# A cross-attention and maxout kernel: the head in another order, batch 3's x issued later, state reads turned behind the weights

## The chip, the cores and the metric

The kernel runs on one core of a Trainium2 chip. The metric is device time in microseconds (us), the median of several runs. Engines are named as the profile names them: PE (matmuls; PEld is its weight load), DVE (vector), ACT (scalar), POOL and SP. DMAs are issued from POOL, ACT and SP. The kernel keeps 8 PSUM banks: four singles (`b0` to `b3`) and two pairs (`w0`, `w1`).

## The reference

Inputs: `x` (8, 8, 512, 64) and `state` (8, 8, 32, 64), batch, head, row, depth; weights `w1`, `w2`, `w3` (512, 768) and `w_out` (768, 512). In float32:

```python
scores = scale * x @ state.T                    # (B, H, 512, 32), scale = 1/8
a = softmax(scores, -1);  xread = a @ state     # rows of x read the state
scores2 = scale * state @ x.T                   # (B, H, 32, 512)
a2 = softmax(scores2, -1); sread = a2 @ x       # rows of the state read x
t = concat([xread, sread], 2)                   # (B, H, 544, 64)
t = t.transpose(0, 2, 1, 3).reshape(4352, 512)  # one token per row
h = max(max(t @ w1, t @ w2), t @ w3)            # maxout, 768 wide
out = h @ w_out                                 # (4352, 512)
```

## The kernel before, in words

Matmuls run in bf16. The 512 x rows of a batch need no product of their own with the state's values: since `xread @ w = a @ (state @ w)`, the kernel forms `G = state @ w` once a batch (32 rows a head, 3 x 768 columns) and then layer 1 as `G` times the turned softmax weights. The 32 state rows of all batches go through layers 1 and 2 together at the end (`"s"`).

The steps of the program are written by hand as a text, step by step; `perform` runs through it and calls one function a step. Within an engine, instructions run in this written order; between engines they wait for one another by semaphores. In the old kernel there are three texts, `FIRST` (head and batches 0 and 1), `EACH` (once for each of five batches) and `LAST`. Two more strings, `BANKS` and `PAIRS`, give the PSUM bank of each product in turn. The steps, with the lines of their instructions:

- `lst k q`: state of batches 2k and 2k+1 from HBM (L152, 128 KB) on queue `q`. `stc`, `stt`, `stp`: cast it (L217), turn it on PE (L222), place it block-diagonally (L228).
- `lxg b g`, `lx b`: half or all of the x of a batch (L168, L163), cast to bf16 under way, on POOL's queue. `lxu`, `cxu`: the first half uncast on SP's queue, cast by DVE (L176).
- `lw m0 m1 i`: columns 128 x m0 to 128 x m1 of weight i (0 for w1, 1 for w2, 2 for w3), cast under way, on POOL's queue (L179); 128 KB in bf16 for each 128 columns. `lwo`: w_out (L184, 768 KB).
- `busy`: a matmul of zeros (L211) that fills PE's wait at the start.
- `xt`/`xtc`: turn x on PE and copy it (batches 0 and 1, L237, L244); `xtd`: turn x by DMA on SP (L249). `sc`: scores (L262, tile `ps`), `ex`: exponentials on ACT (L269), `sum`: sums and reciprocals on DVE (L276, L278), `wt`: softmax weights (L284) on POOL (P) or DVE (D). `at`/`atc`: turn the weights on PE (L295, tile `pat`) and copy them (L298); `atd`: the same by DMA on SP (L302).
- `pad b`: x beside a column of ones on POOL (L308, L311), used by `sr`, the state read (L327, tile `psr`); `srs`: its division (L337 to L343); `srt`: its turn by DMA on SP (L346); `ap`: its place among the state tokens (L351).
- `g b m`, `gc`: a slice of G on PE, 128 columns of each of the three weights (L363, tile `pg`, 8 matmuls), and its copy (L381). `gr`, `grc`: a run of G columns instead (L403, L406).
- `l1 b m`: a block of layer 1 (L416, three products `pw` of two matmuls, one per weight). `m0`, `ma`, `mb`: copy of the first (ACT, L431), maximum with the second and the third (DVE, L436, L440).
- `l2 b j`, `l2c`: layer 2 (L447, tile `po`, 6 matmuls) and its copy to `osb` (L454); `so`: store (L477). `l2p`, `l2pc`, `sop`: parts of these in the last stage (L462, L466, L472).
- `ones`: a constant, behind a copy that waits for w_out (L194, L195). `look`, `flag`, `vl`, `hold`: a test of the sums that decides on a second pass, which is not run here.

Slice m of G needs the weight columns of slice m from all three weights; `l1 b m` needs that slice and the turned weights of the batch. Each transfer on POOL's queue also waits, before it is issued, for the eighth before it to land.

A batch in the loop is one pass of `EACH`: the runs of G and the scores of the next batch stand between the blocks of layer 1 of this one and layer 2 of the one before.

Of the kernel before, what the change touches and what calls it, by code (L numbers as in the profile page):

```python
# [17 lines left out]
FIRST = """  # L18
    lst 0 A; lxu 0 0 S; zero; clr 0; clr 1; clr 2; clr 3; warm; lxg 0 1; busy 1; xones 1; ident; busy 1;
    lxg 1 0; busy 1; busy 1; stc 0 D; busy 1; busy 1; busy 1; busy 1; busy 1; lxg 1 1; stt 0; busy 2;  # L20
    cxu 0 0 D; xt 0 0; stp 0 A; busy 1; xt 0 1; busy 1; xtc 0 0 D; lw 0 2 1; lw 0 2 2; xtc 0 1 D;
    busy 1; sc 0 0; busy 1; lw 0 1 0; busy 1; sc 0 1; lw 1 3 0; ex 0 0; busy 1; busy 1; xt 1 0; sum 0 0;
    lw 2 3 1; busy 1; ex 0 1; sum 0 1; xt 1 1; busy 1; xtc 1 0 AD; busy 1; lw 2 3 2; busy 1; xtc 1 1 A;
    busy 1; wt 0 0 P; wt 0 1 P; xones 0; sc 1 0; ex 1 0; busy 1; sc 1 1; at 0 0; atc 0 0 A; sr 0;
    busy 1; sum 1 0; lw 3 4 0; at 0 1; lst 1 A; lw 3 6 2; lw 3 6 1; ex 1 1; wt 1 0 D; g 0 0; gc 0 0 D;
    busy 1; sum 1 1; g 1 0; sr 1; atc 0 1 A; lw 4 6 0; wt 1 1 P; at 1 0; srs 0; g 1 1; g 0 1; stc 1 P;
    l1 0 0; gc 1 1 D; gc 1 0 A; g 1 2; g 0 2; atc 1 0 A; busy 1; gc 0 1 A; m0 0 0; at 1 1; lxg 2 1;
    srs 1; ma 0 0; l1 0 1; lxg 2 0; gc 0 2 A; l1 0 2; atc 1 1 D; l1 1 0; m0 0 1; m0 0 2; lwo; m0 1 0;
    gc 1 2 A; mb 0 0; xtd 2; l1 1 1; g 0 3; m0 1 1; lst 3 S; lst 2 A; ma 0 1; gc 0 3 A; g 1 3; pad 2;
    stt 1; gc 1 3 A; mb 0 1; ma 0 2; mb 0 2; ma 1 0; mb 1 0; l1 1 2; ma 1 1; g 0 5; m0 1 2; ones; g 0 4;  # L30
    mb 1 1; stp 1 DA; l1 0 3; gc 0 4 A; ma 1 2; g 1 4; gr 2 1792 2304; gc 0 5 D; m0 0 3; mb 1 2; l1 1 3;
    l1 0 5; gc 1 4 A; gr 2 0 512; g 1 5; m0 1 3; ma 0 3; mb 0 3; ma 1 3; l1 1 4; grc 2 1792 2304 A;
    mb 1 3; m0 0 5; gr 2 1280 1792; stc 2 P; lxg 3 1; gr 2 512 1024; ma 0 5; l1 0 4; stt 2; sc 2 -;
    gc 1 5 A; m0 1 4; grc 2 0 512 D; mb 0 5; lxg 3 0; ma 1 4; grc 2 1280 1792 AD; m0 0 4; ma 0 4;
    mb 0 4; mb 1 4; xtd 3; l2 0 3; l2 0 1; ex 2 -; l1 1 5; stp 2 A; l2c 0 3 D; stc 3 P; l2 0 2; sum 2 -;
    l2c 0 1 D; stt 3; l2 0 0; m0 1 5; ma 1 5; l2c 0 2 A; grc 2 512 1024 D; wt 2 - P; sr 2; mb 1 5;
    srs 2; gr 2 1024 1280; l2c 0 0 D; so 0 0 2 P; lx 4; so 0 2 4 P; stp 3 A; grc 2 1024 1280 A; atd 2;
"""
EACH = """
    pad 1; gr 1 1792 2304; gr 1 0 512; grc 1 1792 2304 AD; l2 -1 0; l2 -1 1; l1 0 0; grc 1 0 512 D;  # L40
    l2c -1 0 A; m0 0 0; sc 1 -; l2 -1 3; gr 1 1024 1280; ex 1 -; xtd 2; gr 1 1280 1792; l2c -1 1 D;
    ma 0 0; gr 1 512 1024; mb 0 0; sr 1; grc 1 1024 1280 A; l1 0 1; l1 0 2; sum 1 -; l1 0 3; srs 1;
    l1 0 5; l2c -1 3 A; m0 0 1; m0 0 2; ma 0 1; mb 0 1; ma 0 2; m0 0 3; mb 0 2; srt -2; ma 0 3;
    wt 1 - P; m0 0 5; mb 0 3; l2 -1 2; grc 1 1280 1792 A; grc 1 512 1024 A; ma 0 5; mb 0 5; l2c -1 2 D;
    l1 0 4; so -1 2 4 P; m0 0 4; ma 0 4; lx 3; mb 0 4; atd 1; ap -2 A; so -1 0 2 P;
"""
LAST = """
    srt 6; l1 7 0; srt 7; l2 6 0; l1 7 2; m0 7 0; l1 7 3; l1 7 4; ap 7 D; m0 7 2; srt 5; ap 6 A; ma 7 0;
    m0 7 3; mb 7 0; ap 5 A; l2c 6 0 D; ma 7 2; l2 6 1; l1s 0; l2 6 2; m0 7 4; mb 7 2; l1 7 1; l2c 6 1 A;
    ma 7 3; m0 s 0; l2c 6 2 A; l1s 2; l1 7 5; ma 7 4; mb 7 4; look; ma s 0; m0 7 1; m0 s 2; mb s 0;  # L50
    so 6 2 3 S; m0 7 5; mb 7 3; l1s 1; ma 7 1; mb 7 1; ma s 2; mb s 2; ma 7 5; m0 s 1; ma s 1; l1s 5;
    so 6 0 1 S; mb 7 5; l2p 7 2 384 512; l1s 3; m0 s 5; ma s 5; mb s 1; m0 s 3; mb s 5;
    l2pc 7 2 384 512 A; l2p 7 0 384 512; l2p 7 3 256 512; sop 7 2 384 512 P; ma s 3; l2p 7 2 128 384;
    mb s 3; l2p 7 0 0 128; l2pc 7 0 0 128 A; l2pc 7 3 256 512 D; l2p 7 1 0 128; l2p 7 3 0 256;
    l2pc 7 0 384 512 D; flag; l2pc 7 1 0 128 A; l2pc 7 2 128 384 A; l1s 4; m0 s 4; l2 6 3;
    sop 7 0 0 128 P; ma s 4; sop 7 0 384 512 P; mb s 4; l2p s 0 256 512; so 6 1 2 P; l2 s 1;
    sop 7 3 256 512 A; l2c 6 3 D; l2p 7 2 0 128; sop 7 1 0 128 S; l2p s 0 0 256; so 6 3 4 A;
    l2pc 7 3 0 256 D; l2pc s 0 256 512 D; sop s 0 256 512 A; l2pc 7 2 0 128 A; l2p 7 1 128 384;
    sop 7 2 0 128 A; l2p 7 0 256 384; l2p 7 1 384 512; l2pc s 0 0 256 A; l2p 7 0 128 256;
    l2pc 7 1 128 384 A; l2c s 1 D; sop 7 3 0 256 S; sop 7 2 128 384 P; l2pc 7 0 256 384 D;  # L60
    sop 7 1 128 384 A; l2pc 7 1 384 512 D; sop 7 1 384 512 A; l2pc 7 0 128 256 D; sop 7 0 128 256 A;
    sos 1 S; sop s 0 0 256 S; sop 7 0 256 384 S; hold; vl;
"""

BANKS = """
# [10 lines left out]
def kernel(  # L76
# [60 lines left out]
    def new(d, b, shape, name, bufs=2):  # L137
        d[b] = work.tile(shape, BF16, tag=name, bufs=bufs, name=name)
# [539 lines left out]
```

## Time and profile before

| what | value |
|---|---|
| runs | 152.47, 152.57, 152.87 us; median 152.57 us |
| span of the profiled execution, first to last instruction | 151.4 us |
| what the median has beyond that span | 1.17 us; the profiled execution's own time is its span and about as much around it |
| PE busy | 146.4 us (97%) |
| DVE, ACT, POOL busy | 118.9 (79%), 82.8 (55%), 57.0 us (38%) |
| DMA moved | 22.29 MB |
| granted TensorE clock | 1.000 |

All waits, chains and rows in this document come from one profiled execution. In the chain, each entry is what released the next one, so the entries of PE that follow each other without another engine between them are PE working at its own pace. "PE pg L363 x16" is sixteen matmuls of line 363. Idle time of other engines counts only where the chain passes through them.

### The profile page before, as it was taken

Reading aid. Unit: us, or ns where it says so; the run is one execution under the profiler, and the core shown is the slowest. Engines: PE = TensorE matmul, PEld = TensorE weight load, DVE = VectorE, ACT = ScalarE, POOL = GpSimd, SP = SyncE. Lnnn points to the kernel's source line nnn. Section 1 sums busy time; section 2 is a strip of 40 time slices with the busy share of each in tenths; the row PEclk is TensorE's granted clock in tenths of the full one; section 3 lists DMA queues with packets and bytes.
Section 4 is the critical chain, followed back from the end, with each engine's and each line's share of the span. In section 5 each row is a group of like instructions: output and inputs, shape, how many; then the busy total and the mean of one; then the engine's idle time right before and its main releaser. Section 6 shows DMA issues by size and latency. Waiting matters only on the chain.

```text
span 151.4 us, 3635 instructions
## 1 busy us (share of the span) xinstructions
PE 146.4 (97%) x1431; PEld 73.8 (49%) x1431; DVE 118.9 (79%) x204; ACT 82.8 (55%) x143; POOL 57.0 (38%) x79
## 2 busy tenths in 40 slices
PE   6999799999999999999999999999999999999992
PEld 2566343335445443544354435443544446679771
DVE  6477698999977898879987988798879887675353
ACT  3368558976364665466646664666466653331220
POOL 6979650561528505540554046414331200001500
PEclk9999999999999999999999999999999999999999
DMA  3999999979737979999589749974503250300455
GB/s 115 211 189 195 207 198 195 151 149 139 139 74 167 230 59 265 129 223 132 155 124 230 144 130 140 232 122 141 218 0 78 68 226 4 122 18 17 175 180 196
DMA packets 39108, 22.29 MB, mean 147 GB/s; under 512 B 23072, under 2 KB 36896, under 8 KB 39088
## 3 DMA queue, kind: packets, MB, share of 16 engines
q0 software_dynamic: 15872, 13.96, 48.7%
q1 hardware_dynamic: 21776, 6.82, 23.4%
q10 hardware_dynamic: 1440, 1.25, 2.7%
q8 instruction: 12, 0.20, 0.5%
q14 instruction: 8, 0.07, 0.2%
HBM read 15.20 MB, written 8.91 MB: 159 GB/s over the span
## 4 chain that ended last, share of the span: by engine, by line
PE 86%; DMA 6%; POOL 4%; issue 1%; DVE 1%; POOLq 0%
PE pw L416 46%; PE po L447 25%; DMA w<-in_moe_w_dram 6%; PE pg L363 5%; PE po L462 4%; POOL w L179 2%; PE ps L262 2%; PE psr L327 2%; POOL x L168 1%; PE pgh L363 1%; PE pt L222 1%; DVE held L522 0%; PE idle L520 0%; PE idle L211 0%; DVE osb L466 0%
## 5 line engine op out<-in xcount | busy, mean ns | idle before, releaser
L416 PE MATMUL pw<-aT,G 128*128 128x512 bf16 x288 | 66.8, 379 | 0.0
L431 ACT CAST t<-pw 128x512 bf16<-128x512 f32 (+1 forms) x54 | 30.4, 564 | 28.9 <-PE pw L416 27.2
L416 PEld LDWEIGHTS <-G 128*128 128x128 bf16 x288 | 27.2, 98 | 33.2 <-issue 1.9
L436 DVE TENSOR_TENSOR t<-t,pw 128x512 bf16<-128x512 bf16 (+1 forms) x54 | 35.4, 655 | 9.5 <-ACT t L431 7.4
L447 PE MATMUL po<-wout,ht 128*128 128x512 bf16 x168 | 39.9, 379 | 0.0
L440 DVE TENSOR_TENSOR ht<-t,pw 128x512 bf16<-128x512 bf16 x48 | 32.9, 687 | 4.3
L447 PEld LDWEIGHTS <-ht 128*128 128x128 bf16 x168 | 15.3, 98 | 19.0 <-issue 1.7
L284 POOL TENSOR_TENSOR a<-e,rden 128x1024 bf16<-128x1024 bf16 (+1 forms) x9 | 14.5, 1620 | 24.1 <-ACT osb L454 11.1
L477 POOL DMA_DIRECT2D out_dram<-osb x13 | 7.4, 572 | 30.5 <-ACT t L431 27.5
L403 ACT CAST G<-pg 128x1024 bf16<-128x1024 f32 (+1 forms) x17 | 14.3, 875 | 1.3 <-PE pg L363 1.3
L311 POOL COPY xp<-x 128x1024 bf16<-128x1024 bf16 x12 | 12.3, 1062 | 5.5 <-DMA x<-in_x_dram 5.5
L454 DVE COPY osb<-po 128x512 f32<-128x512 f32 x16 | 10.9, 684 | 2.4 <-PE po L447 2.3
L276 DVE TENSOR_REDUCE seen<-e 128x32 f32<-128x1024 bf16 (+1 forms) x10 | 10.0, 999 | 3.6 <-ACT e L269 3.6
L403 DVE CAST G<-pg 128x1024 bf16<-128x1024 f32 (+1 forms) x13 | 12.2, 972 | 0.7 <-ACT G L403 0.7
L454 ACT COPY osb<-po 128x512 f32<-128x512 f32 x13 | 7.7, 593 | 8.9 <-PE po L447 8.9
L269 ACT ACTIVATE e<-ps 128x1024 bf16<-128x1024 f32 (+1 forms) x10 | 8.5, 854 | 6.6 <-PE ps L262 6.4
L363 PE MATMUL pg<-w,bd 64*32 64x512 bf16 (+1 forms) x288 | 10.8, 362 | 0.9 <-DMA w<-in_moe_w_dram 0.9
L211 PE MATMUL idle<-zero 128*128 128x512 bf16 x27 | 10.0, 477 | 1.3 <-DVE zero L187 1.3
L472 POOL DMA_DIRECT2D out_dram<-osb x4 | 2.2, 544 | 19.4 <-ACT osb L466 19.4
L381 ACT CAST G<-pg 128x768 bf16<-128x768 f32 x9 | 7.1, 801 | 3.3 <-PE pg L363 3.1
L416 PE MATMUL pw<-atp,w 128*128 128x256 bf16 x72 | 8.7, 272 | 0.0
L416 PEld LDWEIGHTS <-w 128*128 128x128 bf16 x72 | 6.9, 98 | 1.5
(70 smaller groups left out, 116.0 us busy)
## 6 DMA issues: line engine op xcount, KB each, us to landing
out_dram<-osb POOLq DMA_DIRECT2D x12, 512.0 KB, 3.5
x<-in_x_dram POOLq DMA_DIRECT2D x4, 512.0 KB, 7.3
x<-in_x_dram POOLq DMA_DIRECT2D x7, 256.0 KB, 5.5
w<-in_moe_w_dram POOLq DMA_DIRECT2D x4, 256.0 KB, 7.5
w<-in_moe_w_dram POOLq DMA_DIRECT2D x2, 384.0 KB, 7.9
wout<-in_moe_w_out_dram POOLq DMA_DIRECT2D x1, 768.0 KB, 11.6
out_dram<-osb SPq DMA_DIRECT2D x3, 256.0 KB, 2.4
osb<-in_x_dram SPq DMA_DIRECT2D x1, 512.0 KB, 4.0
```

What stands on the lines that cost most here:

```text
L211: nc.tensor.matmul(p, zero[:, 0:128], zero, start=True, stop=True)
L276: nc.vector.reduce_sum(out=den, in_=parity(e[b], g), axis=AX.X)
L284: times[c](out=parity(a[b], g).rearrange("p j g s n -> p j (g s) n"), in0=parity(e[b], g).rearrange("p j g s n -> p j (g s) n"), in1=rdens ...
L311: nc.gpsimd.tensor_copy(out=xp[b][:, :, :, g * (D + 1):g * (D + 1) + D], in_=v[:, g])
L363: nc.tensor.matmul(p(s, g), bd(b, 2 * s + g)[64 * g:64 * g + 64, g, :], f(w_sb[64 * g:64 * g + 64, s]), start=True, stop=True, tile_positi ...
L403: copier[c[g]](out=v[:, g:h], in_=p[:, g:h, 0:c1 - c0])
L416: nc.tensor.matmul(pw[i][:, 0:n], lhs(i, k), rhs(k), start=(k == 0), stop=(k == nk - 1))
L431: nc.scalar.copy(out=t0s[b, m][:, 0:n], in_=open_ps["l", b, m][0][:, 0:n])
L436: nc.vector.tensor_max(t1s[b, m][:, 0:n], t0s.pop((b, m))[:, 0:n], open_ps["l", b, m][1][:, 0:n])
L440: nc.vector.tensor_max(ht[b][:, m, :], t1s.pop((b, m))[:, 0:n], open_ps.pop(("l", b, m))[2][:, 0:n])
L447: nc.tensor.matmul(p, ht[b][:, m, j * 128:(j + 1) * 128], wout_sb[:, m, :], start=(m == 0), stop=(m == NM - 1))
L454: copier[c[i]](out=o[:, j, i * w:i * w + w], in_=p[:, i * w:i * w + w])
```

## The change

The three texts become one, `PLAN`, in which every batch is written out. Three things in it are new.

The head. The 27 zero matmuls become 26, differently spread. The weight loads are issued in another order, batch 1's x is followed by `lw 0 1 0` and the columns of slices 0 and 1; two state loads, `lst 1` and `lst 2`, follow each other on ACT's queue and `lst 3` comes a few steps later (before: one early, two late, of these one on SP's queue). On POOL, softmax weights now stand between the weight loads. On this engine, before (`w1`, `w2`, `w3` name the source; `a` are softmax weights, 251 of batch 0, 332 of batch 1; `st` is the state, `x2` batch 2's x):

```order
L179 DMA w_94<-in_moe_w3_dram 128x4x128
L284 TENSOR_TENSOR a_251<-e_180,rden_221 128x4x128
L284 TENSOR_TENSOR a_251<-e_180,rden_228 128x4x128
L198 MEMSET x0_86 128x64
L179 DMA w_94<-in_moe_w1_dram 128x4x128
L179 DMA w_94<-in_moe_w3_dram 128x4x384
L179 DMA w_94<-in_moe_w2_dram 128x4x384
L179 DMA w_94<-in_moe_w1_dram 128x4x256
L284 TENSOR_TENSOR a_332<-e_255,rden_348 128x4x128
L217 CAST st1_79<-stf1_75 128x512
L168 DMA x2_88<-in_x_dram 128x4x256 x2
L184 DMA wout_95<-in_moe_w_out_dram 128x6x512
```

and in the changed kernel (`a_235` of batch 0, `a_396` of batch 1):

```order
L350 TENSOR_TENSOR a_235<-e_217,rden_222 128x4x128
L237 MEMSET x0_82 128x64
L218 DMA w_90<-in_moe_w3_dram 128x4x128
L218 DMA w_90<-in_moe_w2_dram 128x4x384
L350 TENSOR_TENSOR a_396<-e_268,rden_271 128x4x128
L218 DMA w_90<-in_moe_w3_dram 128x4x384
L207 DMA x2_84<-in_x_dram 128x4x256
L218 DMA w_90<-in_moe_w1_dram 128x4x256
L207 DMA x2_84<-in_x_dram 128x4x256
L257 CAST st_473<-stf1_75 128x512
L257 CAST st_475<-stf2_76 128x512
L223 DMA wout_91<-in_moe_w_out_dram 128x6x512
```

The last 128-column block now comes behind batch 0's first weights, the second 384-column block behind batch 1's; the last w1 block stands between the halves of x 2, and a second cast of a state stands ahead of w_out.

On PE, before, this is the place behind the block `l1 0 0`, the first product of slice 2 (`pg`), with what it waits for (`DMASW` are transfers of POOL's queue):

```order
L416 LDWEIGHTS G_334
L416 MATMUL pw2_427<-aT_277,G_334 128x512 [waits DVE_49]
L363 LDWEIGHTS bd0_82 [waits DMASW7_49,DMASW0_49]
L363 MATMUL pg_436<-w_94,bd0_82 32x384 [waits Activation_49]
L363 LDWEIGHTS bd0_82
```

and in the changed kernel the place behind `l1 0 2`, the first product of slice 3:

```order
L478 LDWEIGHTS G_381
L478 MATMUL pw2_512<-aT_309,G_381 128x512 [waits DVE_49]
L428 LDWEIGHTS bd0_78 [waits DMASW7_49,DMASW3_49,DMASW2_49]
L428 MATMUL pg_522<-w_90,bd0_78 32x384 [waits Activation_49]
L428 LDWEIGHTS bd0_78
```

In the old order PE does, from slice 0 on: `g 0 0; g 1 0; sr 1; at 1 0; g 1 1; g 0 1; l1 0 0; g 1 2; g 0 2; at 1 1; l1 0 1; l1 0 2; l1 1 0; l1 1 1; g 0 3; g 1 3`. In the new: `g 0 0; g 1 0; sr 1; sr 0; g 0 1; l1 0 0; at 1 1; at 1 0; g 1 1; l1 0 1; g 0 2; l1 1 0; g 1 2; stt 1; l1 0 2; g 0 3; g 1 3`, with one slice product at a time between blocks. The copies of the slices are on ACT but for half of one (before: ACT and DVE).

Batch 3's x (`lxg 3`) is issued behind `ones`, which waits for w_out, and behind `pad 2`; before, behind `ones` and a cast, with `pad 2` ahead of `ones`. Layer 2 of batches 0 and 1 and the runs of G of batches 2 and 3 are mixed in another order up to `sr 3`.

The loop. On SP, the turn of a state read (`ats`) stands behind the turn of the weights (`aT`). Before, from batch 2's weights on:

```order
L302 DMA_TRANSPOSE aT_880<-a_823 128x8x128
L249 DMA_TRANSPOSE xT_972<-x4_90 128x16x128
L346 DMA_TRANSPOSE ats_100<-sr_403 128x128
L302 DMA_TRANSPOSE aT_1123<-a_1089 128x8x128
L249 DMA_TRANSPOSE xT_1217<-x5_91 128x16x128
L346 DMA_TRANSPOSE ats_100<-sr_467 128x128
```

and now:

```order
L292 DMA_TRANSPOSE xT_1027<-x4_86 128x16x128
L367 DMA_TRANSPOSE aT_1119<-a_1085 128x8x128
L411 DMA_TRANSPOSE ats_96<-sr_392 128x128
L292 DMA_TRANSPOSE xT_1195<-x5_87 128x16x128
L367 DMA_TRANSPOSE aT_1363<-a_1329 128x8x128
L411 DMA_TRANSPOSE ats_96<-sr_389 128x128
```

The turn of batch 3's weights (`aT_1119`) has changed places with the first `ats`. Behind `sr 3` PE's steps are the same ones in the same order as before, and ACT places a state read (`ap`) one batch later.

In the code: SBUF buffers come from a table `PLACES` instead of a rotation; `st` has two buffers instead of four; the four groups of 128 rows of a batch stand in another order in the weights (`turned`, `tokens`), which the exponentials' output pattern makes and layer 2 undoes. Some new functions (a turn of the states by DMA, scores turned the other way) are not called. The diff, its tables cut:

```diff
-FIRST = """
+PLAN = """
...
-    stt 1; gc 1 3 A; mb 0 1; ma 0 2; mb 0 2; ma 1 0; mb 1 0; l1 1 2; ma 1 1; g 0 5; m0 1 2; ones; g 0 4;
...
+    gc 1 2 A; m0 0 2; g 0 3; g 1 3; stp 1 DA; ma 0 2; mb 0 2; gc 0 3 AD; l1 1 1; m0 1 1; ma 1 1; gc 1 3 A;
...
-    st = [data.tile([128, 4, 2, D], BF16, name=f"st{k}") for k in range(B // 2)]
+    st = {}
...
+    def buffer(shape, dtype, tag, key, name=None):
+        n = places[tag][str(key)] if places else str((B if key == "s" else key) % 2)
+        return work.tile(shape, dtype, tag=tag + n, bufs=1, name=name or tag)
...
     def states_cast(k, c):
+        st[k] = buffer([128, 4, 2, D], BF16, "st", k)
         copier[c](out=st[k], in_=st_f[k].unsqueeze(2).to_broadcast((128, 4, 2, D)))
...
+    def turned(j):
+        return j % 2 * 2 + j // 2
...
     def exps(b, g=None):
-        nc.scalar.activation(out=parity(e[b], g), in_=open_ps.pop(("s", b, g)), func=AF.Exp, scale=scale)
+        new(e, b, [128, J, 2, HS, Ns], "e")
+        nc.scalar.activation(
+            out=parity(e[b], g).rearrange("p (c i) g s n -> p i c (g s n)", i=2),
+            in_=open_ps.pop(("s", b, g)).rearrange("p (i c) g s n -> p i c (g s n)", i=2),
+            func=AF.Exp, scale=scale)
...
-                        p[32 * s:32 * s + 32, g], e[b][:, j, g, s, :], both,
+                        p[32 * s:32 * s + 32, g], e[b][:, turned(j), g, s, :], both,
...
-    def g_run(b, c0, c1):
-        new_g(b)
+    def g_run(b, c0, c1, apart=False):
         n = c1 - c0
-        if n > 256:
+        if n > 256 and not apart:
...
+    def tokens(b, j):
+        k = j if b == "s" else turned(j)
+        return slice(k * 128, k * 128 + 128)
...
-            nc.tensor.matmul(p, ht[b][:, m, j * 128:(j + 1) * 128], wout_sb[:, m, :],
+            nc.tensor.matmul(p, ht[b][:, m, tokens(b, j)], wout_sb[:, m, :],
...
-    perform(FIRST)
-    for b in range(2, B - 1):
-        perform(EACH, b)
-    perform(LAST)
+    perform(PLAN)
```

More of the change, by code (lines that the diff above doesn't have):

```diff
@@ L254, in scores @@
     def scores(b, g=None):
-        if not g:
-            new(e, b, [128, J, 2, HS, Ns], "e")
         gs = (0, 1) if g is None else (g,)
@@ L280, in weights @@
     def weights(b, g, c):
-        if not g:
-            new(a, b, [128, J, 2, HS, Ns], "a")
+        new(a, b, [128, J, 2, HS, Ns], "a")
         n = 2 if g is None else 1
@@ L306, in pad @@
     def pad(b):
[L307 removed]
+        new(xp, b, [128, HS, J, 2 * D + 2], "xp")
         nc.gpsimd.memset(xp[b][:, :, :, D:D + 1], 1.0)
```

241 lines of the change are left out of this document (148 added, 93 removed), and 3 rows, old and new, of the table BANKS.

## The prediction

> **What bounds the kernel now.** I read the profile's page first, then the chain of work that ended last in order of time, then PE's instructions of the first 19 us, then the DMA issues one by one.
>
> ```profile
> span 151.4 us, 3635 instructions
> PE 146.4 (97%) x1431; PEld 73.8 (49%) x1431; DVE 118.9 (79%) x204; ACT 82.8 (55%) x143; POOL 57.0 (38%) x79
> PE 86%; DMA 6%; POOL 4%; issue 1%; DVE 1%; POOLq 0%
> ```
>
> The last row is the chain: 86% of the span is PE. In order of time (start, duration, work) it shows where the rest lies:
>
> ```profile
> 8.17 9.70 DMA w<-in_moe_w_dram
> ...
> 17.91 0.52 PE pg L363 x16
> 18.43 0.32 PE idle L211
> 18.75 0.22 PE pat L295 x4
> 18.97 5.20 PE pw L416 x24
> 24.17 0.45 PE pg L363 x16
> 24.62 0.33 PE pt L222 x4
> 24.95 1.40 PE pw L416 x6
> ...
> 35.51 0.47 PE ps L262 x16
> ...
> 47.72 0.47 PE ps L262 x16
> ```
>
> Up to 17.87 us the end is set by a weight block issued at 8.17 that landed 9.70 us later; from there the chain is PE's own work without a hole until the last output copies. So what counts is how much useful PE work is done by the time the weights stop holding PE, and whether the new order opens a hole later. From `sr 3` on (the state read of batch 3) PE's steps stand in the same order in both kernels, the last stage included, so a shift gained or lost by then is carried to the end unchanged.
>
> PE's head, row by row:
>
> ```profile
> 13.35 0.36 PE L363 MATMUL pg<-w,bd 64*32 64x384 bf16 x8
> 14.24 0.63 PE L327 MATMUL psr<-x,e 128*32 128x128 bf16 x32
> 14.80 0.40 PE L295 MATMUL pat<-ident,a 128*128 128x128 bf16 x4
> 15.13 0.52 PE L363 MATMUL pg<-w,bd 64*32 64x384 bf16 x16
> 15.58 1.47 PE L416 MATMUL pw<-aT,G 128*128 128x512 bf16 x6
> 17.91 0.52 PE L363 MATMUL pg<-w,bd 64*32 64x384 bf16 x16 [0.86 <-DMA w<-in_moe_w_dram]
> ```
>
> The starts give the pace: one slice product of 8 costs half of 15.58 - 15.13, 0.225; a state read 14.80 - 14.24 = 0.56; the turn of half a batch's weights 0.22 (chain, 18.75); a block of layer 1 (6 matmuls) 1.30 (5.20/4), or 1.40 next to a slice product (chain, 24.95). Between 13.35 and 18.75 PE did six slice products, one state read, one turn and one block: 1.35 + 0.56 + 0.22 + 1.30 = 3.4 of 5.4 us. Of the other 2.0 us 0.86 are the wait, 0.3 each two zero matmuls, the rest small steps between kinds of work. The new order does a second state read (0.56) in this stretch, which lay ahead of it before, so about 1.4 us is all that it can win here.
>
> **When the weights land.** Issues on POOL, then ACT, and for single transfers the time from issue to landing (last column):
>
> ```profile
> 4.40 4.54 POOL L179 DMA_DIRECT2D w<-in_moe_w_dram  x6
> 12.13 3.04 POOL L179 DMA_DIRECT2D w<-in_moe_w_dram  x4
> 18.27 1.56 POOL L168 DMA_DIRECT2D x<-in_x_dram  x2
> 12.26 0.35 ACTq L152 DMA_DIRECT2D stf<-in_state_dram  x1
> 23.33 0.34 ACTq L152 DMA_DIRECT2D stf<-in_state_dram  x1
> w<-in_moe_w_dram POOLq DMA_DIRECT2D x1, 128.0 KB, 7.2
> w<-in_moe_w_dram POOLq DMA_DIRECT2D x1, 128.0 KB, 6.2
> w<-in_moe_w_dram POOLq DMA_DIRECT2D x1, 384.0 KB, 8.6
> x<-in_x_dram POOLq DMA_DIRECT2D x1, 256.0 KB, 6.6
> x<-in_x_dram POOLq DMA_DIRECT2D x1, 256.0 KB, 7.2
> stf<-in_state_dram ACTq DMA_DIRECT2D x1, 128.0 KB, 5.4
> stf<-in_state_dram ACTq DMA_DIRECT2D x1, 128.0 KB, 8.1
> ```
>
> POOL issues one transfer per 0.76 us. The first weight row is the third block of the first row, the last that slice 0 needs: 4.40 + 2 x 0.76 + 7.2 = 13.1. The next two are the first and third of the batch issued from 12.13: 12.13 + 6.2 = 18.33 and 13.66 + 8.6 = 22.26. The halves of batch 2's x land at 18.27 + 6.6 = 24.87 and 19.04 + 7.2 = 26.24. The DMA engines are backlogged: 256 KB take 26.24 - 24.87 = 1.37 us, 128 KB so about 0.69, whenever they were issued.
>
> **The change part by part.**
>
> *Start of the useful work.* Slice 0 needs the same three blocks behind the same x, in another order; the third again lands at 13.1. One weight product moves from POOL to DVE, state reads move behind slice 0. I start slice 0 at 13.2 (13.35 before; bounds 13.1 and 13.5). The 26 zero matmuls lie ahead of that and cost nothing while the landing covers them; the two that stood behind 13.35 are gone.
>
> *The old wait.* Two blocks of layer 1 (0 0 and 0 1) now stand ahead of slice 2. PE's sum from 13.2: slices 0 and 1 of both batches 0.9, two state reads 1.12, two turns 0.44, two blocks 2.6 to 2.8: slice 2 comes up at 18.3 to 18.5. Its last block is now the tenth transfer of POOL's queue; the tenth landed at 18.33 before. The wait of 0.86 goes, 0 to 0.1 stays.
>
> *What is late next.* The slice after that, `g 0 3`, needs both 384 KB blocks. PE has until then two more slice products 0.45, two blocks 2.6 to 2.8, the turn of state 1 0.33: it is there at 21.7 to 22.1. Before, the second of these blocks landed at 22.26, and PE came for it at 24.17 only. Now two state loads, not one, are issued by ACT ahead of it, and its own issue waits on POOL behind batch 1's weights (the backlog hides that). One more 128 KB costs between 0 and 0.69 us; I take the middle, 0.35, since no row shows which goes first: landing 22.6, PE starts at 22.65 (17.91 was 0.04 behind its landing).
>
> *What that is worth.* Here the new order has done all that the old one had done at 24.17, less the block 1 1 (1.30), and the turn of state 1 besides (0.33): the old one stood there at 24.17 - 1.30 + 0.33 = 23.20. Gain 23.20 - 22.65 = **0.55 us**; 0.25 if the state load costs 0.69, 1.1 to 1.5 if the landing does not hold PE.
>
> *The last block of w1* (slices 4 and 5) is now issued behind the first half of x 2 and so lands where the other half of that pair of issues did, 24.87 + 0.35 = 25.2. PE wants it 0.45 + 2.6 after 22.65, at 25.7. Hidden by 0.5; a PE not held at slice 3 would wait here, so the gain ends near 1.1.
>
> *Copies of slices.* ACT takes eleven and a half of twelve:
>
> ```profile
> L381 ACT CAST G<-pg 128x768 bf16<-128x768 f32 x9 | 7.1, 801 | 3.3 <-PE pg L363 3.1
> ```
>
> A block whose slice copy queues behind a copy of the block before can wait up to one copy, 0.80, at each of four blocks; the nearest row, four blocks in 5.20, shows no such wait. I take 0.1, inside the spread of 21.7 to 22.1; up to 0.5 of it the landing swallows.
>
> *x 2's turn by DMA, w_out, x 3:*
>
> ```profile
> 26.38 4.75 SPq L249 DMA_TRANSPOSE xT<-x  x1
> xT<-x SPq DMA_TRANSPOSE x1, 8.3
> 26.35 2.05 POOL L311 COPY xp<-x 128x1024 bf16<-128x1024 bf16 x2 [5.51 <-DMA x<-in_x_dram]
> 31.42 0.19 POOL L194 COPY last<-wout 128x1 bf16<-128x1 bf16 x1 [3.02 <-DMA wout<-in_moe_w_out_dram]
> 32.25 1.50 POOL L168 DMA_DIRECT2D x<-in_x_dram  x2
> x<-in_x_dram POOLq DMA_DIRECT2D x1, 256.0 KB, 4.7
> 37.76 1.80 SPq L249 DMA_TRANSPOSE xT<-x  x1
> xT<-x SPq DMA_TRANSPOSE x1, 4.3
> ```
>
> x 2 lands 0.35 later, its turn ends at 26.7 + 8.3 = 35.0. The scores of batch 2 (35.51 before) have a block of layer 2 (1.30) and a turn (0.22) more ahead of them and two runs of G (0.28 each) less: 35.51 - 0.55 + 0.96 = 35.9. Cover 0.9. w_out lands at 31.42 + 0.35 = 31.8; x 3 is issued behind it and behind pad 2 (2.05 + 0.2), its second half at 34.8 instead of 33.0. It lands at 34.8 + 4.7 = 39.5 and is turned by 43.8. The scores of batch 3 (47.72 before) now stand ahead of a block of layer 1: 47.72 - 0.55 - 1.30 = 45.9. Their cover shrinks from 5.7 us (37.76 + 4.3 against 47.72) to 2.1 and holds: cost 0. Once it is gone, every us is a us of PE.
>
> *Loop and end.* On SP the turn of a state read now follows the turn of the weights, which ends the sooner; PE waited for neither in the chain, and its order there is unchanged: 0.
>
> Sum: 151.4 - 0.55 = 150.85 us of span. The median of the runs shown, 152.57, lies 1.17 above the span of the profiled execution; with the same 1.17 outside it, **152.0 us**.
>
> **A rule weighed.** The state load issued at 23.33 took 8.1 us and landed at 31.4, together with w_out, which had been issued before it; the one of 12.26 landed at 17.7, beside the weight block of 8.17. So a state load seems to wait its turn behind what was issued earlier. The Trainium skill, "DMA: Bandwidth & Descriptors", section on queues, rings and completion order, states otherwise: each DMA engine alternates between the queues that have work, packet by packet, which would let a load on ACT's queue pass POOL's backlog. By that rule the second state load costs the weights its full share, and the gain would be 0.25 or less; the 5.4 and 8.1 us speak against it.
>
> **The rivals.**
>
> 1. *The landing does not hold PE.* The second state load slips behind, and the block lands at 22.0 rather than 22.26, as PE comes. PE is then held only by w1's last block: gain 0.9 to 1.4, 151.2 to 151.7 us. For it: nothing but one state load is added ahead of that block. Against: 22.26 is measured. 0.15.
>
> 2. *No change.* State loads take turns with the weights: the 384 KB block lands at 22.95, and the third state load, which ACT now issues behind the copy of the fourth slice, at about 18, delays w1's last block by another 0.69: 24.87 + 1.38 = 26.25 against PE at 23.0 + 3.05 = 26.05. Gain 23.20 - 22.99 - 0.24, about 0: 152.3 to 152.8 us. For it: ACT issues all three loads while the weights are under way. Against: the 8.1 us. 0.15.
>
> 3. *Slower: batch 3's scores wait for x 3.* The first turn took 8.3 us beside other transfers, the second 4.3 on idle engines. If x 3's takes 8.3 too, the scores wait: 39.5 + 8.3 = 47.8 against 45.9, 1.9 us lost, 1.35 net, 153.9 us. It decides from a turn later than 45.9 + 0.55. w_out landing late does the same, since it is issued behind two casts that wait for state loads. For it: the cover falls by 3.6 us. Against: no other transfer is due at 39 to 44 us. 0.23.
>
> **How the numbers follow.** 0.3% (0.46 us) is about what a measurement of this kernel can tell from no change. Forecast 0.47, with 151.7 to 152.4 as its own range: 0.33 of it faster by over 0.46, 0.14 within. Rival 1 is faster (0.15); of rival 2, 0.13 is within and 0.02 slower; rival 3 is slower (0.23). That makes 0.48, 0.27, 0.25. The range runs from a little below rival 1, 151.1, to 153.4, the lower part of rival 3; what lies above is about 0.15.
>
> **What would show it.** In the changed kernel's chain the DMA entry should end near 22.6 instead of 17.9, PE waiting 0.4 to 0.9 us at a slice product of 16, and no wait at 17 to 19; then PE without a hole, the turn of x 2 landed by 35.9 and that of x 3 by 45.9, and the last PE row about 0.55 earlier. The prediction is wrong if that block lands outside 22.0 to 23.0, if PE waits on ACT's slice copies for over 0.5 us, or if a scores instruction (`ps`) waits for a DMA.

## The result

The changed kernel takes 153.25 us (median of 22 runs, 152.53 to 154.08) against 152.80 us of the kernel before in the same measurement (22 runs, 152.05 to 154.20): ratio 1.0031, 95% interval 1.0016 to 1.0046. It is slower by about 0.45 us; the forecast was 0.55 us faster. Measured twice more, next to the experiments, the same kernel gave 1.0066 (1.0042 to 1.0089, 6 runs) and 1.0015 (0.9998 to 1.0032, 12 runs); why the six runs lie higher is not shown. Runs in which the granted clock was lower (0.979 to 0.989), or which took over 1.5% more than the fastest run of the same kernel, count neither in the ratios nor in the medians.

The page of the changed kernel, its top and the chain's shares:

```profile
span 152.0 us, 3635 instructions
...
PE 146.2 (96%) x1430; PEld 73.2 (48%) x1430; DVE 117.8 (78%) x204; ACT 83.6 (55%) x142; POOL 55.7 (37%) x78
...
PE 82%; DMA 8%; DVE 3%; issue 3%; POOL 3%; POOLq 0%
```

PE's share of the chain has fallen from 86% to 82%, and DVE and "issue" have risen from 1% to 3% each. The chain of the changed kernel in the order of time (start, duration, work) shows the first place:

```profile
5.96 7.22 DMA w<-in_moe_w_dram
...
13.32 0.52 PE pg L428 x16
...
18.67 0.27 PE pg L428 x4
18.94 0.73 issue
19.67 0.34 PE pg L428 x4
...
23.40 0.45 PE pg L428 x16
```

The old wait for slice 2's weights is gone, as forecast: PE comes to that product (line 428) at 18.6 us and its weights are there. But in the middle of its eight matmuls PE stands still, and the profile sees nothing that it waits for:

```profile
18.60 0.34 PE L428 MATMUL pg<-w,bd 64*32 64x384 bf16 x4
19.67 0.34 PE L428 MATMUL pg<-w,bd 64*32 64x384 bf16 x4 [0.73 <-issue]
19.95 1.47 PE L478 MATMUL pw<-aT,G 128*128 128x512 bf16 x6
```

The chain gives 0.73 us to it; from the start of this product to the next block it is 19.95 - 18.60 = 1.35 us where 0.29 is usual, so it costs 1.06. So PE is at `g 0 3` at 23.3, where the prediction had 22.65, though the 384 KB block had landed (14.29 + 8.0 = 22.3).

The second place, in the same chain, and PE's row for it:

```profile
36.35 0.69 DVE osb L527
...
37.07 1.30 DVE bd L272 x2
...
38.41 0.69 DVE osb L527
39.10 1.14 DVE seen L343
...
40.76 0.11 POOL a L350
...
42.70 4.54 DMA aT<-a
```

```profile
46.42 0.63 PE L306 MATMUL ps<-bd,xT 128*128 128x64 bf16 x16
47.29 1.47 PE L478 MATMUL pw<-aT,G 128*128 128x512 bf16 x6 [0.23 <-DMA aT<-a]
```

The first block of layer 1 of batch 2 (`l1 2 0`) waits for the turn of batch 2's weights (`atd 2`, tile aT). PE's scores of batch 3 take 0.47 and end at 46.42 + 0.47 = 46.89, the block starts at 47.29: it costs 0.40 us. The DVE rows are what stands ahead of it: two output copies and two state copies, then the row sums, then the product on POOL, then the turn, which took 4.5 us. In the kernel before, the same turn took 2.7 us, and PE came to the block at 46.27 without a wait:

```profile
41.60 1.23 SPq L302 DMA_TRANSPOSE aT<-a  x1
aT<-a SPq DMA_TRANSPOSE x1, 2.7
46.27 1.46 PE L416 MATMUL pw<-aT,G 128*128 128x512 bf16 x6
```

From there on both kernels are alike: the passes of the loop are 15.25 us in both.

### The profile page after: what moved, and what is told of

Read it like the earlier page. It is cut to its first block, busy times and chain, and to the rows that moved or that the text cites. A ratio compares the mean times of both kernels' runs of the same rounds, so it can differ in the third digit from the quotient of the medians.

```text
span 152.0 us, 3635 instructions
## 1 busy us (share of the span) xinstructions
PE 146.2 (96%) x1430; PEld 73.2 (48%) x1430; DVE 117.8 (78%) x204; ACT 83.6 (55%) x142; POOL 55.7 (37%) x78
## 4 chain that ended last, share of the span: by engine, by line
PE 82%; DMA 8%; DVE 3%; issue 3%; POOL 3%; POOLq 0%
PE pw L478 46%; PE po L515 21%; PE pg L428 5%; DMA w<-in_moe_w_dram 5%; PE po L533 4%; DMA aT<-a 3%; PE psr L392 2%; PE ps L306 1%; POOL w L218 1%; POOL x L207 1%; DVE osb L527 1%; DVE bd L272 1%; PE pgh L428 1%; DVE seen L343 1%; DVE held L594 0%
## 5 line engine op out<-in xcount | busy, mean ns | idle before, releaser
L350 POOL TENSOR_TENSOR a<-e,rden 128x1024 bf16<-128x1024 bf16 (+1 forms) x8 | 13.5, 1690 | 28.0 <-ACT osb L527 11.5
L467 ACT CAST G<-pg 128x1024 bf16<-128x1024 f32 (+1 forms) x18 | 16.1, 924 | 3.6 <-PE pg L428 3.6
L527 ACT COPY osb<-po 128x512 f32<-128x512 f32 x14 | 8.3, 592 | 10.0 <-PE po L515 10.0
L527 DVE COPY osb<-po 128x512 f32<-128x512 f32 x15 | 10.3, 688 | 4.3 <-PE po L515 4.2
L428 PE MATMUL pg<-w,bd 64*32 64x512 bf16 (+1 forms) x288 | 11.3, 362 | 1.2 <-issue 0.7
L250 PE MATMUL idle<-zero 128*128 128x512 bf16 x26 | 8.9, 448 | 1.4 <-DVE zero L226 1.3
L445 ACT CAST G<-pg 128x768 bf16<-128x768 f32 (+1 forms) x12 | 9.1, 778 | 1.8 <-PE pg L428 1.8
L467 DVE CAST G<-pg 128x1024 bf16<-128x1024 f32 (+1 forms) x10 | 9.7, 1001 | 0.0
L428 PEld LDWEIGHTS <-bd 64*32 64x32 bf16 x336 | 3.4, 89 | 9.1 <-issue 8.0
```

The costliest lines, as they stand in the source:

```text
L350: times[c](out=parity(a[b], g).rearrange("p j g s n -> p j (g s) n"), in0=parity(e[b], g).rearrange("p j g s n -> p j (g s) n"), in1=rdens ...
L428: nc.tensor.matmul(p(s, g), bd(b, 2 * s + g)[64 * g:64 * g + 64, g, :], f(w_sb[64 * g:64 * g + 64, s]), start=True, stop=True, tile_positi ...
L445: copier[c[g]](out=G[b][:, g:h, :, m * 128:m * 128 + 128], in_=p[:, g:h, 0:384].rearrange("p g (i f) -> p g i f", i=3))
L467: copier[c[g]](out=v[:, g:h], in_=p[:, g:h, 0:c1 - c0])
L527: copier[c[i]](out=o[:, j, i * w:i * w + w], in_=p[:, i * w:i * w + w])
```

## Experiments

Every run is compared with the kernel before, on the same chip. "The changed kernel" is the kernel of the profile above.

**The kernel before once more, unchanged.**

> The kernel before, unchanged, profiled once more. Theory (the 0.86 us that PE waited for slice 2's weights are more than that wait usually is): the wait at the slice product of 16 is 0 to 0.6 us this time, and the span is about 151.0. Rival (the wait is the same each time): 0.8 to 0.9 us, span 151.4.

Measured: 152.97 us, ratio 1.0012 (0.9993 to 1.0031), span 150.8. Its chain, which starts with the landing of x:

```profile
3.66 6.46 DMA x<-in_x_dram
...
15.98 1.40 PE pw L416 x6
17.38 0.45 PE pg L363 x16
...
23.57 0.45 PE pg L363 x16
```

No wait at the slice product of line 363: it follows the block without a hole. In this execution the kernel before stands at the slice product that was at 24.17 already at 23.57. So the 0.86 us that the prediction set out to win are not a fixed cost of the kernel. In a third profile with the same head (run e10_state_turn_only, below) the wait was there again:

```profile
8.17 10.23 DMA w<-in_moe_w_dram
...
18.45 0.52 PE pg L363 x16
```

**The changed kernel twice more, unchanged.**

> The changed kernel, unchanged, profiled once more. Theory (the 0.73 us hole at slice product g 0 2 is a late landing of PE's instructions that happens in some executions, the wait for the turn of batch 2's weights is the rule): no hole, first block of layer 1 of batch 2 waits 0.2 to 0.6 us for the turn, span 151.2 to 151.4, ratio 1.003. Rival (the hole is the rule): hole of 0.7 us again, span 151.9.

> The changed kernel, unchanged, next to e8_load_earlier. Theory: no hole or a late landing somewhere in the head, the turn of batch 2's weights 4.5 us with its last two packets behind PE's 16 KB, a wait of 0.2 us and more at the block of layer 1, ratio 1.003 to 1.007. Rival (the wait is chance): the turn takes 2.7 us, no wait, ratio 1.000.

Measured: 153.87 us, ratio 1.0066, span 152.3; and 153.10 us, ratio 1.0015, span 150.9. The hole of 0.73 us was in neither. The wait at `l1 2 0` was in both. a_again first, PE, POOL and the landing of that POOL issue:

```profile
23.67 0.52 PE L428 MATMUL pg<-w,bd 64*32 64x384 bf16 x16 [0.63 <-ACT bd L272]
47.58 1.47 PE L478 MATMUL pw<-aT,G 128*128 128x512 bf16 x6 [0.19 <-DMA aT<-a]
```

```profile
14.94 0.81 POOL L218 DMA_DIRECT2D w<-in_moe_w_dram  x1
```

```profile
w<-in_moe_w_dram POOLq DMA_DIRECT2D x1, 384.0 KB, 8.6
```

The first row is `g 0 3` with a wait of 0.63 us. The profile puts it down to an ACT copy, but that copy makes state diagonals which slice 3 does not use; the 384 KB block, which it does use, landed at 14.94 + 8.6 = 23.5 to 23.6. This is the wait that the prediction forecast for 22.6, in one execution of three, and later. The same block landed at 22.3 in the first profile and at 14.21 + 7.3 = 21.5 in a_third.

a_third had neither, and still waited for the turn. Its PE row, the turn's time to landing, and the DMA queues between 44 and 47 us:

```profile
46.14 1.47 PE L478 MATMUL pw<-aT,G 128*128 128x512 bf16 x6 [0.24 <-DMA aT<-a]
```

```profile
aT<-a SPq DMA_TRANSPOSE x1, 4.6
```

```profile
q8 instruction: 1, 0.02, 2.0%
q1 hardware_dynamic: 2, 0.00, 0.1%
```

The turn (queue q1) has two packets left in this stretch, and one packet of instructions (q8, 16 KB) lies there too. The trace's single packets show how these belong together:

```
run                      turn issued  its other packets  16 KB load       its last two packets  time to landing
before                   41.60        42.78 to 43.88     43.99 to 45.14   with the others       2.7
b_again                  41.00        42.18 to 43.29     43.43 to 44.79   with the others       2.7
the changed kernel       42.70        43.87 to 44.97     45.23 to 46.15   46.14                 4.5
a_again                  43.03        44.21 to 45.31     45.52 to 46.45   46.44                 4.5
a_third                  41.54        42.71 to 43.82     44.06 to 45.01   44.99                 4.6
e1_sum_first             41.25        42.43 to 43.52     43.66 to 45.00   with the others       2.7
e2_store_behind          42.14        43.31 to 44.41     44.63 to 45.58   45.56                 4.5
e6_sum_first_6_less      41.37        42.55 to 43.67     43.84 to 45.11   with the others       2.7
e8_load_earlier          41.82        42.99 to 44.31     41.64 to 42.96   with the others       2.9
e10_state_turn_only      42.13        43.31 to 44.41     44.54 to 45.79   with the others       2.7
```

In every profile of this table where the turn took 4.5 or 4.6 us, 1054 of its 1056 packets are through in 1.1 us, and the last two, 4 bytes each, follow right behind the 16 KB packet. With 2.7 us they don't. (In e3_block_ahead the load came 0.5 us behind the turn: 2.7. In e4, e5 and e9 the load or a store lay among the turn's packets: 3.6, 5.7 and 4.7.) It is close: the load starts 0.11 to 0.17 us behind the data where the turn took 2.7 us, 0.21 to 0.26 where it took 4.5 or 4.6. What puts the two packets behind the load in the one group and not in the other is not shown. The Trainium skill, "DMA: Bandwidth & Descriptors", section on queues, rings and completion order, states that the write which signals completion lands only after every earlier write of that DMA engine, of its other queues too; the table agrees, if the 4-byte packets are such writes, which their size and place suggest. So the turn lands 1.8 us later, and its lead in the new order (issued 4.19 us ahead of PE's need; 4.67 in the kernel before) no longer covers that.

**Batch 2's row sums first.** One output copy moves from DVE to ACT, behind the exponentials:

```
-    stp 2 AD; l2 0 3; l1 1 5; l2c 0 3 D; ex 2 -; sum 2 -; grc 3 1792 2304 A; ...
+    stp 2 AD; l2 0 3; l1 1 5; ex 2 -; sum 2 -; l2c 0 3 A; grc 3 1792 2304 A; ...
```

> Changed kernel, one copy moved: the copy of a layer-2 output of batch 0 that stands on DVE ahead of batch 2's row sums goes to ACT, behind batch 2's exponentials. Theory (the turn of batch 2's weights comes late): the sums start at about 38.4 instead of 39.02 us, the turn is issued at about 42.1 instead of 42.70 and lands by 46.7; PE's first block of layer 1 of batch 2 no longer waits for it (0.40 us idle and 0.17 of refill), so the kernel is 0.5 us faster than the changed one, about as long as the kernel before (ratio 1.000). Rival (the wait is not the cost, something else gives it back): ratio stays 1.003. PE's hole at 18.94 us stays in both.

Measured: 152.78 us, ratio 1.0008 (0.9987 to 1.0029), span 150.7. The turn is issued at 41.25 and lands after 2.7 us; the chain passes the block without a wait:

```profile
44.34 1.40 PE po L512 x6
45.74 0.47 PE ps L303 x16
46.20 1.30 PE pw L475 x6
```

By the ratios (1.0008 against 1.0031) that is 0.35 us less than the changed kernel, where 0.5 was expected; their intervals overlap. There was no hole in this profile, against the expectation. Two things changed for the turn here, its time of issue and its 2.7 us, and the run does not part them.

**The store and x 4 behind.** `so 0 0 2 P; lx 4;` go behind `so 0 2 4 P;`.

> Changed kernel, POOL's order: the store of the first half of batch 0's output and the load of x 4 go behind the store of the second half, which waits for an output copy at about 47.2 us, so that nothing else is under way while batch 2's weights are turned by DMA. Theory (that turn takes 4.5 us instead of 2.7 because of the store and the load beside it): it takes 2.7 to 3.2 us, lands by 46.0, PE does not wait, ratio 1.000 against the kernel before. Rival (the turn is slow by itself): it takes 4.5 us, PE waits 0.4 us as before, ratio 1.003. x 4 comes 3 us later; its turn has that much to spare in both.

Measured: 154.00 us, ratio 1.0093 (1.0059 to 1.0126), span 152.8. With nothing of POOL's queue under way the turn of batch 2's weights still took 4.5 us: the store beside it is not what makes it slow. The kernel is slower for a reason that the expectation had excluded: x 4, loaded 3 us later, delays its own turn on SP, and behind that the turn of batch 3's weights.

```profile
57.70 5.18 DMA aT<-a
62.88 0.04 issue
62.93 1.24 PE pw L475 x5
```

**The turn later.** `pad 3` goes ahead of `wt 2 - P` on POOL.

> Changed kernel; on POOL the padded copy of x 3 (2.2 us) goes ahead of the product that makes batch 2's weights, so that these, their turn and the block of layer 1 behind it come later: the copy can start at 39.1 us, when x 3 has landed, and ends at 41.3; the product started at 40.76, or at about 40.1 where PE has no hole. Theory (the turn is on the path in the changed kernel): 0.5 to 1.3 us slower than the changed kernel, ratio against the kernel before 1.006 to 1.012, PE waiting 1.0 to 1.8 us at that block. Rival (it is beside the path): ratio 1.003 as without the edit.

```profile
48.47 0.82 PE L475 MATMUL pw<-aT,G 128*128 128x512 bf16 x3 [2.02 <-DMA aT<-a]
```

Measured: span 153.2, PE idle 2.2 us ahead of the block, counted as the 0.40 above; two runs count, 154.25 and 154.97 us, too few for an interval. PE came to the block 3.61 us behind the issue of the turn, 0.58 sooner than in the changed kernel, and the turn landed after 5.7 us instead of 4.5, beside the store, which was now earlier. Together that is the growth of the wait, more than the 1.0 to 1.8 us expected: the turn is on the path.

**Two blocks ahead of the slices.** In the head, `l1 1 0` moves ahead of `g 0 2` and `l1 1 1` ahead of `g 1 2`.

> Changed kernel, PE's order in the head: block 1 0 of layer 1 stands ahead of slice product g 0 2, and block 1 1 ahead of g 1 2. Theory (PE runs out of instructions: 16 KB of them land by DMA too late, when it has begun 449 recorded instructions, wherever in the order that is): the hole falls into block 1 0, at about 19.5 us, and is 0 to 0.3 us instead of 0.73, since a block has 12 instructions in 1.3 us and a slice product 16 in 0.23; g 0 3 starts at about the same work 0.4 to 0.6 us sooner, ratio 1.000 against the kernel before. Rival (the hole belongs to slice product g 0 2, its weights or its banks): it stays 0.7 us between the fourth and fifth matmul of g 0 2, ratio 1.003.

```profile
23.05 1.74 PE L475 MATMUL pw<-aT,G 128*128 128x512 bf16 x6 [0.94 <-ACT t L490]
```

Measured: 153.88 us, ratio 1.0083 (1.0057 to 1.0109). Inconclusive on the hole: the 16 KB load came at 14.5 us, when it does not matter, and there was no hole to move. The order cost 0.94 us of its own, since PE waited for ACT's copies of the blocks that now follow each other more closely.

**Sixteen instructions more.** Eight zero matmuls of 64 columns ahead of the first slice product (`tiny 8;` behind `at 0 1;`).

> Changed kernel with 8 more zero matmuls, of 64 columns, ahead of the first slice product, where PE waits 0.49 us for the weights anyway: 16 more instructions of PE. Theory (PE runs out of instructions): the hole begins 16 instructions earlier, inside block 0 1 of layer 1, at about 17.6 us, and ends at 19.2 to 19.7 as before; the kernel is 0 to 0.7 us slower than the changed one (ratio 1.003 to 1.008 against the kernel before). Rival (the hole belongs to g 0 2): it stays at the same four matmuls, 0.7 us, ratio 1.003.

Measured: 152.84 us, ratio 1.0004 (0.9981 to 1.0027), span 151.0. Again no hole, so no answer on it; neither theory's ratio came. What the trace shows besides is that the load at the turn came at 42.5 us (44.1 to 45.5 in the three profiles of the changed kernel), the turn took 3.6 us, and PE did not wait for it.

**Row sums first, six zero matmuls less.**

```
-    xt 1 1; lw 3 4 0; ... busy 1; busy 1; busy 1; sum 0 1; sc 1 0; ... at 0 0; busy 1; ... sc 1 1; busy 1; busy 1; at 0 1; g 0 0;
+    xt 1 1; lw 3 4 0; ... sum 0 1; sc 1 0; ... at 0 0; ... sc 1 1; at 0 1; g 0 0;
```

> Run e1_sum_first with six of the 26 zero matmuls taken out, those between the last turn of batch 1's x and the first slice product. Theory (in that run PE reached the first slice product at 13.54 us without a wait, behind zero matmuls that were no longer covered): the first slice product starts when its weights land, 13.1 to 13.4, the rest follows, 0.2 to 0.4 us less than e1_sum_first, ratio against the kernel before 0.997 to 0.999. Rival (the weights' landing holds PE at the same time anyway): as e1_sum_first, 1.000 to 1.001. The 12 instructions less also let PE run out of instructions later, if it does.

Measured: 152.60 us, ratio 0.9989 (0.9971 to 1.0007), span 150.8. The lowest ratio of all kernels run, under the first two measurements of the changed kernel by more than the intervals, but not separable from the third or from the kernel before. The first slice product started at 13.40, at its weights. In this execution the 16 KB load of the head came late, at 17.26 us (17.20 in the profile with the hole; 13.4 to 16.1 in all others), and PE's rows have a small hole, in another place of the order:

```profile
18.68 0.36 PE L425 MATMUL pg<-w,bd 64*32 64x384 bf16 x8
18.97 1.63 PE L475 MATMUL pw<-aT,G 128*128 128x512 bf16 x6
20.54 0.36 PE L425 MATMUL pg<-w,bd 64*32 64x384 bf16 x8
```

A block that takes 1.47 us takes 1.63: its matmuls stop for 0.16 us, up to 19.57. Counted from the start, the first instruction behind the hole is the same in both executions: PE's 223rd weight load, at 19.67 and at 19.57 us. In the order these are two places, the middle of slice product `g 0 2` and the block `l1 1 0` behind it, 12 instructions apart, as many as the six zero matmuls have. So the hole goes with the number of instructions, not with the work, as it would if PE had run out of instructions; no record shows what PE waits for. Both times it goes on 2.3 to 2.5 us after the start of the 16 KB packet. That rests on two executions. The Trainium skill, "Runtime: NRT & Kernel Launch", section on instruction fetch mechanics, has each engine refill its instructions in 16 KB blocks through a DMA queue of its own, at a cost that is mostly hidden; here it was not hidden in these two of the eleven profiles of the changed kernel and its variants.

**The load elsewhere.** Each zero matmul is cut in two of 256 columns, 52 instructions more at the same time of PE:

```
         for _ in range(n):
-            nc.tensor.matmul(p, zero[:, 0:128], zero, start=True, stop=True)
+            for c in (0, 256):
+                nc.tensor.matmul(p[:, c:c + 256], zero[:, 0:128], zero[:, c:c + 256], start=True, stop=True)
```

> Changed kernel with each of the 26 zero matmuls cut into two of 256 columns: PE's time ahead of the first slice product stays, but PE has issued 52 instructions more, so that each 16 KB load of its instructions is asked for 52 instructions earlier in the order. Theory (the turn of batch 2's weights takes 4.5 us where its last two packets wait for a 16 KB load of PE's instructions, which PE asks for at about its 940th recorded instruction, 44.5 us, while the turn's data move from 43.9 to 45.0): the load is asked for at about 41 us and is over by 43.9, the turn takes 2.7 to 3.6 us, PE does not wait for it, 0.4 to 0.6 us less than the changed kernel, ratio 0.999 to 1.001 against the kernel before. Rival (the turn is slow for another reason): 4.5 us and a wait again, ratio as a_third.

Measured: 153.03 us, ratio 1.000 (0.998 to 1.002), span 150.7. The load came at 41.64 and was over by 42.96, before the turn's packets; the turn, issued at 41.82, took 2.9 us:

```profile
aT<-a SPq DMA_TRANSPOSE x1, 2.9
```

```profile
45.55 0.63 PE L307 MATMUL ps<-bd,xT 128*128 128x64 bf16 x16
46.02 1.46 PE L479 MATMUL pw<-aT,G 128*128 128x512 bf16 x6
```

PE goes from the scores to the block without a wait, with no step of DVE, ACT, POOL or SP moved. Here only the number of PE's instructions differs from a_third, where the turn, issued 0.28 us sooner, took 4.6 us. From the first slice product to the last instruction e8 takes 137.20 us and a_third 137.63, 0.43 more. In the medians the two don't part (153.03 and 153.10); the trace carries the finding.

**Both cures.** e6 with its 20 zero matmuls cut in two.

> Run e6_sum_first_6_less with its 20 zero matmuls cut in two as well, 28 instructions more than the changed kernel ahead of the first slice product. Theory (batch 2's weights are early, PE's instruction load is asked for before the turn, and PE does not run out of instructions in the head): no wait from the first slice product to the last stage, span 150.3 to 150.7, ratio 0.996 to 0.999 against the kernel before. Rival (nothing was left to gain in e6): 0.998 to 1.000.

Measured: 153.05 us, ratio 1.0005 (0.9982 to 1.0028), span 150.7: not below e6. The profile has no wait on the path from the first slice product to the last stage, and yet the ratio is that of the kernel before. The load did not clear the turn here: it lay among the turn's packets, and the turn, issued at 41.18, landed after 4.7 us, just as PE came to the block at 45.96. The profiled execution took 152.45 us, less than the median; what makes the others longer no profile shows.

**One part of the change alone.** In the kernel before, `srt -2` goes behind `atd 1` in the loop.

> The kernel before with one part of the change alone: in the loop, the turn of a state read stands behind the turn of the weights on SP, in all five passes. Forecast of the prediction: no effect, ratio 1.000, the loop's pace stays 15.25 us. Rival (the state turn ahead of the weights held PE): the loop is faster, ratio below 0.997.

Measured: 153.55 us, ratio 1.0036 (1.0013 to 1.0058), span 152.2. Neither expectation. The edit was not the part alone: the copy that places the state read (`ap -2 A`) still stood right behind, so that ACT, and DVE and PE behind it, waited for the landing of the state turn,

```profile
58.27 2.34 DMA ats<-sr
60.61 0.02 issue
60.63 0.03 ACT atp L351
```

and one pass took 15.47 us. The changed kernel places each state read a pass later. Besides, this profile has the weight wait of 0.76 us shown above. So what the order on SP does alone was not measured; in the changed kernel the passes stayed at 15.25.

## Why the prediction was wrong

Put side by side, the head's profiles say it best. "Work point" is the start of the row of `g 0 3` (for the old order that row less 1.30 for the block 1 1 and plus 0.33 for the turn of state 1, as in the prediction); "between" is the time from the first slice product to it, "to the end" from the first slice product to the last instruction:

```
run                   first slice  work point  between  to the end  waits between
before                13.35        23.13       9.78     138.08      0.86 weights of slice 2
b_again               13.68        22.53       8.85     137.17      none
e10 (head of before)  13.98        23.67       9.69     138.20      0.76 weights of slice 2
the changed kernel    13.32        23.33       10.01    138.67      1.06 hole
a_again               13.93        23.67       9.74     138.37      0.63 weights of slice 3
a_third               13.23        22.17       8.94     137.63      none
e1_sum_first          13.54        22.49       8.95     137.20      none
e2_store_behind       13.79        22.74       8.95     139.04      none
e4_16_more            13.83        22.78       8.95     137.21      none
e5_turn_later         13.79        22.74       8.95     139.39      none
e6_sum_first_6_less   13.40        22.45       9.05     137.44      0.16 hole
e8_load_earlier       13.51        22.46       8.95     137.20      none
e9_both               13.46        22.41       8.95     137.20      none
```

Without a wait both orders need the same, 8.85 and 8.95 us (the new one does a state read more behind the first slice product, the old one two zero matmuls), and to the end both need 137.2. (e2, e5 and e10 wait elsewhere, as told above.) So the new head wins nothing by its order; it changes which late landing meets PE. And what the changed kernel's three profiles have beyond 137.2 is a wait in the head (1.06, 0.79, none) and the wait for the turn (0.40, 0.35 and 0.40).

The runs bear this out. Five variants with the new head and no wait for the turn (e1, e4, e6, e8, e9) gave ratios of 0.9989 to 1.0008; their 56 runs together come to 0.9999 (0.9990 to 1.0008), the 40 runs of the changed kernel to 1.0030 (1.0019 to 1.0041; means against the kernel before beside them, with two standard errors). Two of the five, e4 and e8, differ from the changed kernel by zero matmuls alone: 0.9999 (0.9986 to 1.0012) together. Zero matmuls also move PE's loads in the head, so a part of this can be the hole's.

The turn's lead fell for a reason that lies in PE's order: between the scores of batch 2 and the block `l1 2 0` PE now has a block of layer 2 and the turn of a state less to do, and two runs of G and batch 3's scores more. In b_again these scores and the block are 10.92 us apart:

```profile
34.75 0.63 PE L262 MATMUL ps<-bd,xT 128*128 128x64 bf16 x16
45.67 1.46 PE L416 MATMUL pw<-aT,G 128*128 128x512 bf16 x6
```

In a_third the block is due when batch 3's scores (the second row) are done, 0.47 behind their start, which is 10.52 us behind the scores of batch 2:

```profile
35.22 0.63 PE L306 MATMUL ps<-bd,xT 128*128 128x64 bf16 x16
45.27 0.63 PE L306 MATMUL ps<-bd,xT 128*128 128x64 bf16 x16
```

The turn is issued at 41.00 and 41.54, 6.25 and 6.32 us behind the scores of batch 2. So its lead is 4.67 us in the old order and 4.20 in the new, enough for a turn of 2.7 us and not for one of 4.5.

The steps of the prediction, one by one:

- *What that is worth* (gain 0.55) failed. The 23.20 at which "the old one stood" (23.13 by the rows) is one execution with a late landing. In b_again it stood at 22.53, and there the gain is nothing. The mechanism was right (a wait for weights at slice 2), its size was taken as fixed and differs between executions: 0.86, 0.76 and 0 us.
- The sentence that sets the median 1.17 above that span, "with the same 1.17 outside it", hid this; so does the line on it in the table of the kernel before. In the runs beside all experiments 1.75 to 1.98 us lie outside the span. The profiled execution of 151.4 so took about 153.2 us, 0.6 over its median; its wait of 0.86 is more than that. Against 153.2 the same gain of 0.55 would have given about 152.7, no change.
- *The change part by part* lacks a term: the turn of batch 2's weights. The text follows x 2's and x 3's turns and leaves this one out. Its lead fell to 4.2 us, and the turn took 4.5. PE waited there in all three profiles of the changed kernel; e1, e4 and e8 take the wait away, e5 makes it 2.2 us. This is what turned no change into slower, as far as the runs can tell. That this turn can take 4.5 us the one profile of that time does not show (2.7): the term was left out, but its size could not have been read there. *Loop and end: 0* itself holds: 15.25 us per pass.
- *What is late next* was the exception: the 384 KB block does hold PE at `g 0 3`, in a_again. Its landing was forecast at 22.6 (22.0 to 23.0) and was 22.3, 23.5 and 21.5 in the changed kernel, and 21.2 to 22.0 in its eight variants; PE waited for it in one profile of eleven. The 22.26 from which it was worked out was also one execution: in b_again that block landed at 21.3.
- *Start of the useful work*, 13.2 with bounds 13.1 and 13.5: 13.32, 13.23, and 13.93 in a_again. The bounds were too narrow for a landing that moves by 0.7.
- *The old wait*: slice 2 came up at 18.60 (forecast 18.3 to 18.5) and did not wait. *Last block of w1*: landed at 15.83 + 9.4 = 25.2, as forecast, hidden. *Copies of slices*: no wait on ACT in the changed kernel. *x 2's turn, w_out, x 3*: the scores waited for neither; rival 3 did not come, and rival 2 neither. What rival 1 assumes, a landing that does not hold PE, is the rule (ten profiles of eleven); its gain did not come, since the 23.20 was not the rule. The slower side won by a wait that none of the three names.
- *A rule weighed*: the state load issued at 17.85 landed after 4.9 us, at 22.75, ahead of the weight block issued at 15.83, which landed at 25.2. So a load on ACT's queue passes POOL's backlog, as the Trainium skill, "DMA: Bandwidth & Descriptors", section on queues, rings and completion order, has it; the 5.4 and 8.1 us from which the prediction argued against the rule don't show that a load waits its turn. With the rule the prediction would have come to a gain of 0.25 or less, nearer to the result, but by a landing at 22.95, later than in ten of eleven profiles: that would have been luck.

What stays open: how often the hole comes, why the turn's last packets fall behind the load in every profile of the changed kernel, and how the 0.45 us of the medians divide between the turn and the landings in the head. The turn's 0.35 to 0.40 alone would be most of it.

## What to carry to other kernels

Before a wait is counted as gain, find out whether it is there in every execution: compare the profiled execution's own time (span plus what the runs have outside it) with the median, and take the wait at what is left. When work moves in front of a step, list every transfer that the step needs and its lead, then and now; the one that was left out here had 0.5 us less lead, and its landing varied by 1.8 us. Where PE is the bound and its order is dense, the loading of its own instructions is one more transfer on that list: here such a load stood ahead of the turn's last packets, and late ones stood beside the two holes.

## Hardware, not expected

- PE's instructions come in loads of 16 KB, 12 for its 2,874 recorded instructions, each a single packet of 0.9 to 1.9 us. 52 instructions more moved the loads earlier by 1.2 us (the first) and 2.4 us (the one at the turn; e8 against a_third). Where the first load started at 17.2 or 17.3 instead of 13.4 to 16.1 us, beside the loading of weights, PE stood still at the same instruction number; that cost 1.06 and 0.16 us.
- A turn by DMA of 256 KB landed after 2.7 us or after 4.5 to 4.6 us, according to whether its last two packets of 4 bytes came before or behind such a load (nine profiles; 2.9 us with the load ahead of all its packets).
- The same 384 KB block, issued at 14.2 to 14.9 us by the same code, took 6.7, 7.3, 8.0 and 8.6 us to land in four executions (e1, a_third, the changed kernel, a_again), and 6.6 to 7.5 in the other seven, issued at 14.4 to 15.1.
